# A pre-LN attention and SwiGLU block on one core: two-part opening, normalising tile by tile behind an estimated end, Newton steps in one piece, and which engine copies the last query block and the row sums

## The chip, the core and the metric

The program runs on one core of a Trainium2 chip. Its engines work in parallel, each through a queue of its own in program order: PE (TensorE, matrix products; PEld is its loading of stationary operands), DVE (VectorE), ACT (ScalarE), POOL (GpSimd) and SP (SyncE, which here only issues DMAs). They wait for each other through semaphores. The metric is device time in microseconds (us) of one execution; less is better. A row that begins with L99 tells of line 99 of the kernel.

## The reference

A transformer block on 2048 tokens of width 640, with 32 heads of 20 and a feed-forward width of 1728, all in fp32:

```
def _A_ref(x, wqkv, wo):
    qkv = (x @ wqkv).reshape(B, S, 3, H, Dh).transpose(2, 0, 3, 1, 4)
    q, k, v = qkv[0], qkv[1], qkv[2]
    p = softmax(einsum("bhqd,bhkd->bhqk", q, k) * Dh ** -0.5)
    o = einsum("bhqk,bhkd->bhqd", p, v)
    return o.transpose(0, 2, 1, 3).reshape(B, S, D) @ wo
def _B_ref(x, w_gate, w_up, w_down):
    return (silu(x @ w_gate) * (x @ w_up)) @ w_down
h  = x + _A_ref(layernorm(x), A_wqkv, A_wo)
h2 = h + _B_ref(layernorm(h), B_w_gate, B_w_up, B_w_down)
```

## The kernel before

Tokens are cut into four chunks of 512 (`c`, `NC = 4`), a chunk into four tiles of 128 (`TPC = 4`), the heads into eight groups of four (`g`, `NG = 8`). fp32 products are made of three products of rounded parts: each operand is split into `hi` (a rounded copy) and `lo` (the rest), and hi·hi, hi·lo and lo·hi are summed in PSUM. A `split` is therefore one copy (ACT) and one subtraction (DVE or POOL).

**Stage 1, projections** (to about 324 us). For each chunk: layer norm of four token tiles, turning them (`flip`) to put the features on the partitions, then ten query and key blocks and eight value blocks. A block is `rounds` (L594): 15 products of 64 rows each and, 20 products later, their 15 other halves. Between the rounds `visit` slips in other work by a model of the engines' clocks (`clock`, advanced by `takes` with estimated ns): chiefly the *early maxima* (`max_four`, L212, L224, L234), which compute row maxima of scores that the softmax needs and would else have to be made later; they read keys and queries back from DRAM into `raw` tiles. A maximum's reduction on DVE frees one of the five PSUM banks that its products use, and PE's queue is in order: a late reduction holds PE up.

The layer norm of chunk c+1 runs inside the blocks of chunk c as a list of steps `lns`, made by `norm`: four `stats` (two bn_stats and one bn_aggr on DVE), the reciprocal square root by three Newton steps (`rstd_steps`: two guess operations on DVE, twelve small ones, two to a list entry, on POOL), then four `apply` (L501, DVE), which normalise a tile in place. `norm_step` takes one entry from the list; it is called at most once per `visit` while `steps_due` lasts, and in a loop at the start of each block. When the last POOL entry has been issued, `x_there` is set to the estimated end of the chain plus `CHAIN` (3000 ns), and no entry is taken before that time of the model. POOL's queue also holds the splits of query and key blocks and the DMAs that store them (L566), from which SP's loads of `raw` (L152) follow.

For chunk 0 nothing can run ahead: the norm is written out in order (four stats, 14 Newton operations on DVE, four `apply`), then the turning (`flip_tokens`, L555), and the first two blocks (`first_blocks`, L647) in pieces of 256 columns. Before it PE does three products that nobody reads (L747), on the last x tile. `fill_ones` (L141) sets rows of the stacked keys to one on POOL. The last query block of chunk 3 is copied from PSUM by ACT (L679), split by ACT and POOL and stored through SP.

**Stage 2, attention** (to about 1460 us): 32 units `u` (group and chunk), each 16 key tiles `kt`. Per kt: four score products (`ps_one`, L1217, four banks in turn), four exponentials on ACT (L1223), eight products with the values into `acc` (L1227, called W here), and, while any are left, three late maxima (L245 on PE, L251 on DVE). W lags two kt behind the scores. After a unit's last W, `row_sums` copies `acc` to SBUF: 384 of 512 columns on ACT (L1238), then 128 on DVE (L1239). `acc` has one bank, so the next unit's first W waits for both.

**Stage 3**: output projection and the feed-forward part; its norms use the same `rstd_steps`, taken five (`moments`) or seven (`late_tokens`) operations at a time.

## Time and profile before

| what | us |
|---|---|
| runs: median (lowest to highest of 3) | 2030.67 (2030.37 to 2032.34) |
| the profiled execution | 2030.02 |
| its span, first to last instruction | 2028.2 |
| PE busy in the span | 2003.0 |
| mean granted PE clock | 0.999 |

The profile follows one execution. Busy times are unions of an engine's records. PE's matmuls are pipelined and their ends are modelled, so that PE can be told busy while it is held up for a few tenths of a us; starts of successive matmuls are the finer measure. The windows view gives, for each stretch of time, its length, each engine's busy time with the number of instructions, then the granted clock, the busy share of the DMA engines and GB/s. The waits view reads: who waited for whom, us in total, times, longest. The timeline reads: start, length, engine, line, operation, output and inputs, shapes, number merged, and in brackets the engine's idle time before it and what ended it.

### The profile page before, as it was taken

What the parts mean: (1) busy time and instruction counts of PE and PEld (TensorE: products, weight loads), DVE (VectorE), ACT (ScalarE), POOL (GpSimd) and SP (SyncE); (2) the same over time, 40 slices, a digit from 0 to 9 for tenths busy, and PEclk for the clock granted to TensorE, in tenths of its full rate; (3) what the DMA queues carried; (4) which work ended last, traced back from release to release, by engine and by line L of the source; (5) the groups of instructions that cost most, each with busy time, mean ns of one, the idle gap of its engine ahead of it and who ended that gap; (6) DMA issues with size and microseconds to landing.
All of it is one profiled execution on the core that took longest, in us unless ns stands there. A gap on an engine that the chain in (4) does not pass through costs nothing.

```text
span 2028.2 us, 40006 instructions
## 1 busy us (share of the span) xinstructions
PE 2003.0 (99%) x14300; PEld 1249.2 (62%) x14300; DVE 1610.5 (79%) x2858; ACT 1436.5 (71%) x2828; POOL 785.9 (39%) x1152
## 2 busy tenths in 40 slices
PE   8999999999999999999999999999999999999998
PEld 6989996333343433443333443345598888888888
DVE  5677778888999898989998989876388666676677
ACT  4677778999999999999999999987634222212221
POOL 6464423343352444343500011011146444844555
PEclk9999999999999999999999999999999999999999
DMA  7787563443534544535512132221158654974642
GB/s 243 245 254 260 175 209 83 127 138 105 184 109 126 164 128 131 160 122 175 158 49 78 28 83 61 87 62 55 51 194 296 216 185 158 354 266 155 205 149 93
DMA packets 199343, 310.38 MB, mean 153 GB/s; under 512 B 53744, under 2 KB 87856, under 8 KB 198120
## 3 DMA queue, kind: packets, MB, share of 16 engines
q1 hardware_dynamic: 192552, 284.21, 43.4%
q0 software_dynamic: 6496, 23.60, 4.0%
q8 instruction: 114, 1.87, 0.4%
q14 instruction: 85, 0.70, 0.1%
q10 hardware_dynamic: 96, 0.00, 0.0%
HBM read 208.11 MB, written 99.19 MB: 152 GB/s over the span
## 4 chain that ended last, share of the span: by engine, by line
PE 89%; DVE 1%; DMA 1%; issue 1%; ACT 1%; SPq 0%; POOL 0%; DVEq 0%; ACTq 0%; POOLq 0%
PE acc L1227 25%; PE ps_a L1397 15%; PE ps_one L1217 15%; PE ps_max L245 13%; PE ps_b L1491 8%; PE ps_one L594 6%; PE ps_max L212 2%; PE ps_max L948 2%; PE ps_b L948 2%; DMA halves<-j_d 1%; ACT probs L1223 0%; PE ps_max L983 0%; DVE tmp L1612 0%; SPq L1173 0%; SPq L297 0%
## 5 line engine op out<-in xcount | busy, mean ns | idle before, releaser
L1223 ACT ACTIVATE probs<-ps_one 128x512 f32<-128x512 f32 x2048 | 1058.0, 609 | 60.8 <-PE ps_one L1217 35.4
L251 DVE TENSOR_REDUCE mx<-ps_max 128x1 f32<-128x512 f32 x1472 | 924.9, 684 | 92.6 <-PE ps_one L1217 70.8
L1217 PE MATMUL ps_one<-q_stk,k_stk 62*128 62x512 f32 x2048 | 577.9, 447 | 1.0 <-ACT probs L1223 0.8
L1227 PE MATMUL acc<-probs,v_stk 128*32 128x512 f32 x4096 | 545.3, 605 | 1.0
L1217 PEld LDWEIGHTS ps_one<-q_stk,k_stk 62*128 62x128 f32 x2048 | 249.2, 184 | 436.9 <-ACT probs L1223 408.4
L245 PE MATMUL ps_max<-k_stk,q_stk 60*128 60x512 f32 x1472 | 371.6, 425 | 0.0
L245 PEld LDWEIGHTS ps_max<-k_stk,q_stk 60*128 60x128 f32 x1472 | 271.9, 186 | 22.4 <-DVE mx L251 0.9
L1612 DVE TENSOR_TENSOR tmp<-ps_a,tmp 128x512 f32<-128x512 f32 x208 | 141.2, 689 | 120.3 <-PE ps_a L1397 94.6
L234 DVE TENSOR_REDUCE mx<-ps_max 128x2 f32<-128x512 f32 x288 | 180.4, 685 | 66.9 <-PE ps_max L212 63.7
L1227 PEld LDWEIGHTS acc<-probs,v_stk 128*32 128x32 f32 x4096 | 80.7, 108 | 181.6 <-issue 167.1
L224 ACT ACTIVATE ps_max<-ps_max 128x512 f32<-128x512 f32 x288 | 151.7, 584 | 48.4 <-PE ps_max L212 45.6
L1491 PE MATMUL ps_b<-halves,yp 128*128 128x320 f32 x1032 | 179.3, 309 | 2.0 <-DMA halves<-j_d 1.3
L1491 PEld LDWEIGHTS ps_b<-halves,yp 128*128 128x128 f32 x1032 | 165.2, 188 | 18.6 <-POOL yp L90 1.5
L1397 PE MATMUL ps_a<-t,units 128*128 128x512 f32 x624 | 162.7, 396 | 0.2 <-ACT tmp L1625 0.2
L1397 PE MATMUL ps_a<-z,units 128*128 128x512 f32 x516 | 133.9, 394 | 0.0
L90 POOL TENSOR_TENSOR yp<-y,yp 128x256 fp32r<-128x256 f32 x96 | 60.2, 628 | 188.5 <-ACT yp L89 180.2
L1397 PEld LDWEIGHTS ps_a<-t,units 128*128 128x128 f32 x624 | 112.6, 188 | 19.0 <-ACT tmp L1625 0.5
L1264 POOL TENSOR_TENSOR o<-o,rb 128x512 f32<-128x512 f32 x31 | 39.9, 1286 | 199.2 <-DMA q_stk<-m_d 63.5
L1496 DVE TENSOR_TENSOR h<-ps_b,h 128x320 f32<-128x320 f32 x248 | 110.1, 481 | 7.1 <-PE ps_b L1491 5.4
L594 PE MATMUL ps_one<-z_hi,w_lo 64*128 64x512 f32 x380 | 112.6, 393 | 0.0
L594 PE MATMUL ps_one<-z_hi,w_hi 64*128 64x512 f32 x380 | 111.9, 393 | 0.0
L594 PE MATMUL ps_one<-z_lo,w_hi 64*128 64x512 f32 x380 | 111.4, 392 | 0.0
(215 smaller groups left out, 2644.8 us busy)
## 6 DMA issues: line engine op xcount, KB each, us to landing
units<-w_d SPq DMA_DIRECT2D x186, 256.0 KB
w_d<-stage SPq DMA_DIRECT2D x106, 256.0 KB
halves<-j_d SPq DMA_DIRECT2D x70, 320.0 KB
j_d<-stage SPq DMA_DIRECT2D x42, 320.0 KB
k_stk<-k_d SPq DMA_DIRECT2D x64, 160.0 KB
q_stk<-q_d SPq DMA_DIRECT2D x64, 160.0 KB
raw<-k_d SPq DMA_DIRECT2D x62, 160.0 KB
raw<-q_d SPq DMA_DIRECT2D x54, 160.0 KB
```

The costliest lines, as they stand in the source:

```text
L224: nc.scalar.activation(ps, ps, AF.Relu)
L234: nc.vector.tensor_reduce(mx[:, b, :, t, kc], ps.rearrange("p (j n) -> p j n", j=2), axis=AX.X, op=ALU.max,)
L245: nc.tensor.matmul(ps, queries[u][rows, pair, t * P : (t + 1) * P], keys[u // NC][rows, pair, kc * CH : (kc + 1) * CH], start=True, stop=True,
L251: nc.vector.tensor_reduce(mxs[u][:, b, pair, t, kc : kc + 1], ps, axis=AX.X, op=ALU.max)
L594: nc.tensor.matmul(ps, a[rows], b[rows], start=(i == n == 0), stop=(i == 1 and n == last), skip_group_check=True,)
L1217: nc.tensor.matmul(ps, keys[u // NC][rows, p, kt * P : (kt + 1) * P], queries[u][rows, p, :], start=True, stop=True,)
L1223: nc.scalar.activation(probs[p][:, b, :], ps, AF.Exp, scale=scale)
L1227: nc.tensor.matmul(acc[32 * j : 32 * j + 32, :], values[u // NC][:, kt, j * VW : j * VW + 32], probs[j // 2][:, j % 2, :], start=(kt == 0) ...
L1397: nc.tensor.matmul(ps.rearrange("p (t n) -> p t n", t=TPC), w[k][:, i], z[k][:, :, j], start=(first and m == 0), stop=(last and m == len(n ...
L1491: nc.tensor.matmul(ps, a, b, start=(n == 0), stop=(n == len(pairs) - 1))
L1496: nc.vector.tensor_tensor(out=h, in0=ps, in1=h, op=ALU.add)
L1612: add = lambda out, ps, x: nc.vector.tensor_tensor(out=out, in0=ps, in1=x, op=ALU.add)
```

## The change

1. **Opening.** The norm of chunk 0 is made for two halves of two tiles. On DVE: stats of tiles 0 and 1, their Newton steps threaded between the stats of tiles 2 and 3 (`between`); the Newton steps of tiles 2 and 3 go to POOL. Then PE turns tiles 0 and 1, computes columns 0 to 255 of the first two blocks for two of the three products, turns tiles 2 and 3, and does the rest. There are four products for nobody on x tile 0 where there were three on tile 3. One of the two halves of the ones is set by DVE and ACT where POOL did both.
2. **Newton steps.** On DVE one is three operations where it was four (a constant is folded into the guess); on POOL it is as before. `norm` uses POOL for all.
3. **One piece.** When `norm_step` meets a POOL entry it takes all POOL entries at once; `CHAIN` is 5000. The loop at a block's start becomes one step at most. `flip` of a chunk first takes what is left of the list.
4. **Normalising** (`norm_tokens`) for chunks 1 to 3 writes into another tile, whose five pieces of 128 columns lie 129 apart; there are five x tiles where there were four.
5. `LATE` is 4: weight blocks 4 and 5 have their `lo` made by POOL instead of DVE. `AFTER` (5, 6) puts one set of early maxima before group 7's.
6. The **last query block** is copied from PSUM by DVE and split by POOL alone.
7. **Row sums:** ACT copies all 512 columns.
8. Tiles for maxima of later units come from three buffers in turn.

```diff
+        if engine is nc.vector:
+            first = [
+                some(ts, v, var, EPS, -0.5, op0=ALU.add, op1=ALU.mult),
+                some(
+                    ts, r.bitcast(I32), v.bitcast(I32), -0.5, 519526879.0, op0=ALU.mult, op1=ALU.add
+                ),
+            ]
+            again = [
+                some(tt, out=t, in0=r, in1=r, op=ALU.mult),
+                some(tt, out=t, in0=t, in1=v, op=ALU.mult),
+                some(engine.scalar_tensor_tensor, r, t, 1.5, r, op0=ALU.add, op1=ALU.mult),
+            ]
+            return r, first + again * 3
...
-    def stats(pool, src, mv):
+    def stats(pool, src, mv, between=()):
         st = pool.tile([P, 2, 6], F32, name="st")
+        between = list(between)
         for i in range(2):
             nc.vector.bn_stats(st[:, i, :], src[:, i * HALF : (i + 1) * HALF])
+            if between:
+                between.pop(0)()
         nc.vector.bn_aggr(mv, st)
+        for f in between:
+            f()
...
+            if b and others:
+                others[0].memset(ones[:, 0], 1.0)
+                nc.scalar.activation(k[rows, 1], ones[:, 0], AF.Copy)
+            else:
+                nc.gpsimd.memset(ones, 1.0)
...
-        AFTER = 5, 7
+        AFTER = 5, 6
-        LATE, CHAIN = 6, 3000
+        LATE, CHAIN = 4, 5000
...
             takes(engine, ns, clock["PE"])
-            if engine == "POOL" and lns[0][0] == "DVE":
+            if lns and lns[0][0] == "POOL":
+                while lns[0][0] == "POOL":
+                    _, ns, f = lns.pop(0)
+                    f()
+                    takes("POOL", ns, clock["PE"])
                 x_there[0] = max(clock["PE"], clock["POOL"]) + CHAIN
...
+        def norm_tokens(tile, mv, r, t):
+            old = new = xs[tile]
+            if tile >= TPC:
+                old = old.rearrange("p (k n) -> p k n", k=ND)
+                new = xs[tile] = x_tile().rearrange("p (k n) -> p k n", k=ND)[:, :, :P]
+            nc.vector.tensor_scalar(
+                new, old, mv[:, t, 0:1], r[:, t : t + 1], op0=ALU.subtract, op1=ALU.mult
             )
...
             else:
-                nc.scalar.activation(copy[:, :CH], ps, AF.Copy)
+                if sync:
+                    nc.vector.tensor_copy(copy[:, :CH], ps)
+                else:
+                    nc.scalar.activation(copy[:, :CH], ps, AF.Copy)
...
+                    if sync:
+                        nc.gpsimd.tensor_copy(hi[:, :n], copy[:, :n])
+                        nc.gpsimd.tensor_tensor(
+                            out=lo[:, :n], in0=copy[:, :n], in1=hi[:, :n].bitcast(F32),
+                            op=ALU.subtract,
+                        )
+                        return
...
+        for _ in range(4):
+            nc.tensor.matmul(warm, ident, xs[0][:, :CH], start=True, stop=True)
+        r1, steps = rstd_steps(pa, mv[:, :2, 1], 2, "b")
+        r2, others = rstd_steps(pa, mv[:, 2:, 1], 2, "c", nc.gpsimd)
+        for t in range(2):
+            stats(pa, xs[t], mv[:, t, :])
+        for f in steps[:3]:
             f()
+        stats(pa, xs[2], mv[:, 2, :], steps[3:7])
+        stats(pa, xs[3], mv[:, 3, :], steps[7:])
+        for f in others:
+            f()
...
+        first_hi(0)
+        for t in range(2):
+            norm_tokens(t, mv, r1, t)
+            flip_tokens(t)
+            flipped_hi(t)
+        first_hi(1)
+        flipped_lo(0)
+        flipped_lo(1)
+        first_lo(0)
+        first_blocks((0, 0), (0, 1))
+        for t in range(2, TPC):
+            norm_tokens(t, mv[:, 2:], r2, t - 2)
+            flip_tokens(t)
+            flipped_hi(t)
...
                 if clock["PE"] >= x_there[0]:
-                    while steps_due[0] and lns:
-                        steps_due[0] -= 1
+                    if steps_due[0] and lns:
                         norm_step()
...
-        most = 3 * P
-        nc.scalar.activation(o[:, :most], acc[:, :most], AF.Copy)
-        nc.vector.tensor_copy(o[:, most:], acc[:, most:])
+        nc.scalar.activation(o, acc, AF.Copy)
```

What the planner makes of it stands in the engines' orders. First DVE, in the middle of chunk 0's blocks, from the sum over the last key block (`e`) to the early maxima (`mx`); L501 and, in the change, L551 are the normalising of chunk 1's tiles. Before:

```order
L684 TENSOR_TENSOR e_165<-e_165 128x256
L501 TENSOR_SCALAR xt<-xt,mv,r_a 128x640 x4
L234 TENSOR_REDUCE mx_131<-ps_max 128x2 x8
L234 TENSOR_REDUCE mx_135<-ps_max 128x2 x8
L234 TENSOR_REDUCE mx_139<-ps_max 128x2 x8
```

and in the change:

```order
L737 TENSOR_TENSOR e_150<-e_150 128x256
L551 TENSOR_SCALAR xt<-xt,mv,r_a 128x5x128 x3
L261 TENSOR_REDUCE mx_130<-ps_max 128x2 x4
L551 TENSOR_SCALAR xt<-xt,mv,r_a 128x5x128
L261 TENSOR_REDUCE mx_130<-ps_max 128x2 x4
```

Four normalisings ahead of the maxima became three, with the fourth behind two pairs of maxima. For chunks 2 and 3 every one of the four stands alone between maxima in the change.

Second POOL at the same time: the Newton operations of chunk 1 (`t_a`, `r_a`) and the splits and stores (DMA rows) of blocks. Before:

```order
L99 TENSOR_TENSOR r_a<-r_a,t_a 128x4
L90 TENSOR_TENSOR z_lo<-z_lo 128x256
L566 DMA k_d_63<-z_lo 16x2x768
L566 DMA k_d_63<-z_lo 80x2x768
L566 DMA k_d_63<-z_lo 32x2x768
L99 TENSOR_TENSOR t_a<-r_a 128x4
L99 TENSOR_TENSOR t_a<-t_a,v_a 128x4
L566 DMA q_d_59<-e_164 16x2x512
```

and in the change:

```order
L99 TENSOR_TENSOR r_a<-r_a,t_a 128x4
L99 TENSOR_TENSOR t_a<-r_a 128x4
L99 TENSOR_TENSOR t_a<-t_a,v_a 128x4
L99 TENSOR_SCALAR t_a<-t_a 128x4
L99 TENSOR_TENSOR r_a<-r_a,t_a 128x4
L90 TENSOR_TENSOR z_lo<-z_lo 128x256
L615 DMA k_d_63<-z_lo 16x2x768
```

The rows shown in the change are the end of twelve in a row; the split of `z_lo` and its stores stand behind all twelve, where they stood behind four.

Third DVE at the passage from stage 1 to stage 2: the last early maxima (`mx_129`), then the first late ones (`mx_128`). Before:

```order
L234 TENSOR_REDUCE mx_129<-ps_max 128x2 x12
L90 TENSOR_TENSOR m_5512<-ps_max,m_5512 16x128
L234 TENSOR_REDUCE mx_129<-ps_max 128x2 x4
L251 TENSOR_REDUCE mx_128<-ps_max 128x1 x31
```

and in the change:

```order
L90 TENSOR_TENSOR m_5191<-ps_max,m_5191 16x128
L261 TENSOR_REDUCE mx_143<-ps_max 128x2 x14
L261 TENSOR_REDUCE mx_129<-ps_max 128x2 x14
L730 COPY e_150<-ps_one 128x512
L261 TENSOR_REDUCE mx_129<-ps_max 128x2 x2
L280 TENSOR_REDUCE mx_128<-ps_max 128x1 x31
```

The finish of unit 0's maxima (`m`) moved up by a good twenty reductions, the copy of the last query block joined DVE's queue, and a pair of early maxima stands behind it.

More of the change, by code (lines that the diff above doesn't have):

```diff
@@ L171, in load_values, with mx_tile @@
         )
-    mxs = {u: stk.tile([P, 2, 2, TPC, NC], F32, name=f"mx{u}") for u in range(NU)}
+    def mx_tile(u, **tag):
+        return stk.tile([P, 2, 2, TPC, NC], F32, name=f"mx{u}", **tag)
+    mxs = {u: mx_tile(u) for u in range(NU) if u % NC < 2 or u == 2}
     clock = dict.fromkeys(("PE", "ACT", "DVE", "POOL"), 0)
@@ L496, in norm @@
             mv = pa.tile([P, TPC, 2], F32, name="mv")
[L497 to L504 removed]
+            r, steps = rstd_steps(pa, mv[:, :, 1], TPC, "a", nc.gpsimd)
             return (
@@ L520, in flip @@
             if n == 0:
+                while lns:
+                    norm_step()
                 zs[c] = z_tiles(c)
@@ L741, in tile_block @@
         load_x(0)
-        fill_ones(k_stk[0])
+        fill_ones(k_stk[0], nc.vector)
         for i in range(4):
```

67 lines of the change are left out of this document (35 added, 32 removed).

## The prediction

> **What bounds the kernel now.** The page first, then the windows view by stage (us and busy time of PE, PEld, DVE, ACT, POOL), then PE's waits in stage 1.
>
> ```profile
> PE 2003.0 (99%) x14300; PEld 1249.2 (62%) x14300; DVE 1610.5 (79%) x2858; ACT 1436.5 (71%) x2828; POOL 785.9 (39%) x1152
> ...
> 22.00:324.00 302.00, 296.28 (x3379) 279.83 (x3377) 214.69 (x365) 219.57 (x427) 152.20 (x210) 0.99 0.72 228
> 324.00:1460.00 1136.00, 1133.99 (x7884) 469.69 (x7883) 980.45 (x1686) 1074.87 (x2111) 328.37 (x524) 1.00 0.35 107
> ...
> PE ps_two L747 <- DMA xt<-in_A_x: 7.9, 1, 7.9
> PE ps_max L212 <- DVE mx L234: 4.6, 3, 2.4
> PE ps_max L212 <- ACT ps_max L224: 0.8, 2, 0.5
> ```
>
> PE is busy for 99% of the span, so an edit earns only where PE stands still, or where another engine holds up the start of its matmuls without the busy time showing it. In stage 1 PE stands still for 302.00 − 296.28 = 5.7 us, most of it in three waits for reductions of the early maxima. The opening, the passage to stage 2 and the 31 changes of unit are the other places. All sums below are made against the profiled execution, 2030.02 us; the median of the runs shown is 0.65 us above it.
>
> **The norms of chunks 1 to 3.** DVE and PE at chunk 1, a window at the slow clock behind it, and all sixteen normalisings (shortest, median, longest ns):
>
> ```profile
> 58.75 5.01 DVE L501 TENSOR_SCALAR xt<-xt,mv,r_a 128x640 f32<-128x640 f32 x4 [1.68 <-POOL r_a L99]
> 64.41 0.39 PE L212 MATMUL ps_max<-raw 60*128 60x256 f32 x2 [2.40 <-DVE mx L234]
> 66.00:70.00 4.00, 4.00 (x45) 4.00 (x43) 1.44 (x3) 2.01 (x4) 2.63 (x4) 0.60 0.90 323
> ...
> L501 DVE TENSOR_SCALAR xt<-xt,mv,r_a x16: 602/606/2101, 11.7 to 213.6; 128x640 f32<-128x640 f32 x16
> ...
> 50.48 0.20 POOL L99 TENSOR_TENSOR t_a<-r_a 128x4 f32<-128x4 f32 x1
> 51.32 0.20 POOL L99 TENSOR_TENSOR r_a<-r_a,t_a 128x4 f32<-128x4 f32 x1
> 19.54 3.02 DVE L90 TENSOR_TENSOR w_lo<-raw,w_hi 128x640 fp32r<-128x640 f32 x4
> ```
>
> DVE waits 1.68 us for the last Newton operation, then four normalisings take 5.01 us (twice the 4 × 0.606 that they need at the median), and the maxima behind them come late: PE stands still for 2.40 us. Then the granted clock falls to a mean of 0.60 over 4 us with PE busy throughout, which is 4 × 0.40 = 1.6 us of lost work. In the change the twelve Newton operations run in one piece. The first four start from 50.48 to 51.32, 0.28 us apart, so twelve take 3.4 us and end near 53.9; DVE asks at 58.75 − 1.68 = 57.07. The normalisings write five pieces. The trace has none of that form: the lower bound is 0.606, the upper the longest seen, 2.101; I take 0.76, from the four subtractions of 128x640 in 3.02 us, the nearest DVE row of that size. Three in a row are then 2.3 us, ahead of maxima that were held up for 1.68 + 5.01 = 6.7. The 4.4 us gained exceed the 2.40 that PE waited, so the wait goes and the slow clock with it: **−2.4 and −1.6**. What is late next would be the banks behind the three normalisings: 2.3 us of DVE against 1.9 in the planner's estimate, hidden by the reductions that PE has already queued.
>
> On the form: the Trainium skill (VectorE: DVE Perf Modes, Mode 2×_2P) says that this mode needs outermost sizes that are even or equal in source and destination, which five pieces out of a plain row of 640 would not be; and (SBUF — State Buffer, two separate sides) that an operation in that mode and a GpSimd one exclude each other for their whole length. The spread from 602 to 2101 ns agrees with such exclusion; by these pages the new form costs about 0.76 and never waits.
>
> Chunks 2 and 3, by the same views:
>
> ```profile
> 126.56 1.53 DVE L501 TENSOR_SCALAR xt<-xt,mv,r_a 128x640 f32<-128x640 f32 x1 [2.63 <-POOL r_a L99]
> 124.00:130.00 6.00, 4.10 (x42) 3.45 (x38) 3.44 (x5) 3.03 (x7) 5.04 (x9) 1.00 0.89 306
> 203.00:206.00 3.00, 2.70 (x30) 2.35 (x28) 2.01 (x5) 2.27 (x5) 0.46 (x3) 1.00 0.80 264
> 103.00:112.00 9.00, 8.34 (x77) 7.24 (x75) 8.86 (x20) 6.67 (x12) 5.53 (x6) 1.00 0.78 221
> ```
>
> At 126 DVE waits 2.63 us for a Newton chain that POOL had been given in pieces between stores; the first normalising now stands eight reductions later on DVE, some 5 us, and the chain is whole: PE's 6.00 − 4.10 = 1.9 us go, **−1.9**. At 203 the same in small, **−0.3**. At 103 to 112 three stats in a row hold reductions up and PE loses 9.00 − 8.34 = 0.66; the change takes one stat at a time, but that stretch has ACT waits too: between 0 and −0.66, I take **−0.3**. `LATE` gives POOL two subtractions near 20 us, while it waits for the first blocks; at nothing, since DVE's next work there waits for PE. The AFTER order and the later tiles for maxima move no work into a wait that I can find: nothing, with ±1 for what a planner does elsewhere.
>
> **The opening.**
>
> ```profile
> 1.38 7.05 POOL L141 MEMSET k_stk<- 32x4096 f32 x2
> 3.83 0.89 DVE L125 BATCH_NORM_STATS2 st<-xt 128x6 f32<-128x320 f32 x2 [2.95 <-DMA xt<-in_A_x]
> 6.78 0.89 DVE L125 BATCH_NORM_STATS2 st<-xt 128x6 f32<-128x320 f32 x2 [0.83 <-DMA xt<-in_A_x]
> 8.94 0.17 DVE L99 TENSOR_SCALAR v_a<-mv 128x4 f32<-128x4 f32 x1
> 11.74 2.18 DVE L501 TENSOR_SCALAR xt<-xt,mv,r_a 128x640 f32<-128x640 f32 x4
> 12.40 1.86 PE L555 MATMUL ps_wide<-ident,xt 128*128 128x128 f32 x15
> 7.89 4.45 PE L747 MATMUL ps_two<-xt,ident 128*128 128x512 f32 x6 [7.89 <-DMA xt<-in_A_x]
> 22.41 1.43 PE L594 MATMUL ps_one<-z_hi,w_hi 64*128 64x512 f32 x5
> ```
>
> Tile 0 lands at 3.83, tile 2 at 6.78. The ones on DVE (half of what POOL does in 3.5 us, so below 1.8 at its rate) lie before 3.83, their copy on ACT before its first turned tile is there: no cost. From 6.78 DVE now does four bn_stats (0.89 a pair), two aggregates (0.1) and ten small operations (0.2 each, as 14 fill 8.94 to 11.74): 1.8 + 0.2 + 2.0 = 4.0, so the first normalising starts near 10.7, not 11.74, and PE turns from 11.4, not 12.40. But PE's 10.0 us from there to 22.41 grow: its first product needs the turned tile 1 and the second weight block, both through ACT, at about 13.4, so some 0.6 of the 1.0 is given back: **−0.4**, bounds 0 and −1.0. A caution: the four idle products, at 4.45 / 3 each from 3.83, end by 9.8, sooner if the clock rises, and PE then stands still for 1.6 us or more; at chunk 1 a stop of 2.40 brought the slow clock. If it falls here, 1.6 are lost again.
>
> The Trainium skill (TensorE: Matmul & The Clock Gate, Why this matters for your kernels) has the clock fall only for gaps beyond about 3 us. The fall behind 2.40 us differs from it, and the measurement decides; by the page this loss has no chance, and −0.4 stands.
>
> **The changes of unit.** One boundary on PE (W rows), ACT and DVE, and the waits of W for the copy:
>
> ```profile
> 838.03 1.06 PE L1227 MATMUL acc<-probs,v_stk 128*32 128x512 f32 x8
> 840.15 1.07 PE L1227 MATMUL acc<-probs,v_stk 128*32 128x512 f32 x8
> 842.38 1.07 PE L1227 MATMUL acc<-probs,v_stk 128*32 128x512 f32 x8
> 844.60 1.06 PE L1227 MATMUL acc<-probs,v_stk 128*32 128x512 f32 x8
> ...
> 839.56 2.07 ACT L1223 ACTIVATE probs<-ps_one 128x512 f32<-128x512 f32 x4
> 841.48 0.53 ACT L1238 ACTIVATE o<-acc 128x384 f32<-128x384 f32 x1
> 841.85 2.66 ACT L1223 ACTIVATE probs<-ps_one 128x512 f32<-128x512 f32 x5
> 842.04 0.29 DVE L1239 COPY o<-acc 128x128 f32<-128x128 f32 x1 [0.35 <-ACT o L1238]
> ...
> PEld acc L1227 <- DVE o L1239: 13.5, 29, 0.5
> ```
>
> A kt takes 840.15 − 838.03 = 2.12 us; the two around a boundary take 2.23 and 2.22, so each of 29 boundaries costs 0.21. Two things meet there. W waits for the DVE part, which ends at 842.33. And ACT is full: four exponentials fill 839.56 to 841.48, 0.48 each, leaving 2.12 − 1.92 = 0.20 per kt for a copy that takes 841.85 − 841.48 = 0.37. ACT falls 0.17 behind, the fourth score finds its bank still in use, and the next W is late. The change ends the first wait: 512 columns are done by about 842.1, before W's turn at 842.27. It deepens the second: the copy takes 0.48, ACT falls 0.28 behind. If ACT decides, 0.21 becomes 0.31, 29 × 0.1 = +2.9; if W's wait decided, 842.38 − 842.27 = 0.11 goes, −3.2; if all goes, −6.1. Since the second late kt is explained by ACT alone, I take **+2.9**. This edit is the one that speaks against the change.
>
> **The passage to stage 2, and the end of attention.**
>
> ```profile
> 324.19 0.60 ACT L679 ACTIVATE e<-ps_one 128x512 f32<-128x512 f32 x1 [2.08 <-POOL e L90]
> 325.36 2.04 ACT L1223 ACTIVATE probs<-ps_one 128x512 f32<-128x512 f32 x4
> 325.99 0.98 PE L1217 MATMUL ps_one<-q_stk,k_stk 62*128 62x512 f32 x2 [0.83 <-ACT probs L1223]
> 1464.04 1.00 PE L948 MATMUL ps_b<-wo_hi,o_hi 128*128 128x320 f32 x5 [1.07 <-DVE o L1239]
> ```
>
> Without the copy and split of the last query block (324.19 to 325.36) ACT could begin its exponentials up to 1.2 us earlier. But DVE now has that copy (about 0.7) and a pair of early maxima (1.3) behind it, and PE's first late maxima need their banks: from −1.2 to +0.5, I take **−0.2**. At 1464 PE waits 1.07 for ACT's and then DVE's share of the last sums; without the second, **−0.3**. The feed-forward part has three norm operations fewer in each chain and begins its late tokens one step earlier: nothing.
>
> Sum: −2.4 − 1.6 − 1.9 − 0.3 − 0.3 − 0.4 + 2.9 − 0.2 − 0.3 = −4.5, so 2030.02 − 4.5 = **2025.5 us**; bounds of the terms carry it from about 2022 to 2028.5.
>
> **Rivals.** *The unit change gains.* W's wait goes and ACT's lag is absorbed by the four banks: −3.2 in place of +2.9, 2025.5 − 6.1 = 2019.4. For it: DVE's 0.29 lies in series on W's wait, 29 times. Against: the row at 841.85 shows ACT without a pause. *The stalls move.* The planner's clocks err elsewhere, PE finds new waits of 2 us twice, half of the 6.5 of the norms' gain comes back and the idle opening drops the clock (1.6): 2025.5 + 3.2 + 1.6 = 2030.3. For it: the planner was 4 us wrong at chunk 1. *The one piece stops POOL (slower).* Twelve operations, 3.4 us, stand ahead of the splits and stores of two blocks, and SP's loads of `raw` follow those stores:
>
> ```profile
> SPq L152 <- POOL t_a L99: 3.6, 1, 3.6
> ```
>
> SP has waited 3.6 us for such operations once already. If a load lands later than the planner's due time, PE stands for up to 3.4 and the clock falls for 1.6 more, 5.0 a chunk; two chunks would give 2035.5, three 2040.5. It decides once the delay exceeds the slack in the landing times; against it, PE's waits now name no `raw` transfer at all.
>
> **Chances.** Forecast 0.44 (its own range 2022 to 2028.5); the unit change gains 0.18; the stalls move 0.26; POOL stopped 0.12. No more than 0.2% (4.06 us, what a measurement of this kernel can hardly tell from nothing) off 2030.67 is 2026.6 to 2034.7. Of the forecast some three quarters lie below 2026.6 (0.33), all of the second (0.18) and a little of the third (0.03): faster 0.54, same 0.34, slower 0.12. For the range I reach down into the second case and up over the third: 2018.5 to 2031.5.
>
> **What would show it.** Right: no PE wait on L261 above 1 us near 60 and 126; clock 1.00 there; normalisings of 128x5x128 near 0.76 us with no long ones; PE's turning from 11.4; first W of units 2.12 after the one before, but the second W about 2.43 after it. Wrong: W intervals at boundaries of 2.12 twice (second case); PE waits for `raw` (fourth); a granted clock of one half near 11 to 15.

## The result and the profile after

The changed kernel takes 2025.84 us (median of 5 runs, 2022.30 to 2026.28), the kernel before 2032.19 on the same chip (5 runs, 2030.37 to 2033.13): a ratio of 0.9966, 95% interval 0.9955 to 0.9977. It is faster by 0.34%, and the interval lies beyond the 0.2% that the prediction asked for. Predicted were 2025.5 us. The prediction stood against earlier runs of the kernel before (2030.67); beside the changed kernel that kernel was 1.5 us slower, so the medians differ by 6.35 us. In the two profiled executions the span goes from 2028.2 to 2024.0.

The page's busy times and the windows of the two large stages after the change (columns as before):

```profile
PE 2003.7 (99%) x14302; PEld 1242.0 (61%) x14302; DVE 1602.4 (79%) x2816; ACT 1439.9 (71%) x2827; POOL 788.5 (39%) x1166
...
22.00:324.00 302.00, 297.38 (x3393) 279.09 (x3395) 219.69 (x370) 223.49 (x435) 158.23 (x217) 1.00 0.72 228
324.00:1460.00 1136.00, 1134.55 (x7892) 463.13 (x7884) 971.43 (x1647) 1074.83 (x2107) 324.15 (x520) 1.00 0.35 106
```

PE's busy total hides the gain, as it hid the loss: it does the same products, and stands still for less. PE's waits after the change (total, times, longest):

```profile
PE ps_two L805 <- DMA xt<-in_A_x: 4.3, 1, 4.3
...
PE ps_max L569 <- DVE xt L551: 1.8, 2, 1.0
...
PE ps_max L274 <- DVE mx L261: 0.9, 1, 0.9
PE ps_max L239 <- ACT ps_max L251: 0.9, 2, 0.6
...
PE ps_one L1300 <- DMA q_stk<-m_d: 0.6, 1, 0.6
PE ps_max L239 <- DVE mx L261: 0.4, 1, 0.4
```

The last row was the largest of stage 1 before (4.6 us, L212 <- L234). In its place stands a smaller new one: the flips (L569, turning of the next chunk) wait 1.8 us for normalised tiles. DVE and PE around the first of them:

```profile
57.55 0.93 DVE L551 TENSOR_SCALAR xt<-xt,mv,r_a 128x640 f32<-128x640 f32 x1
60.08 1.92 DVE L551 TENSOR_SCALAR xt<-xt,mv,r_a 128x640 f32<-128x640 f32 x2 [1.60 <-issue]
61.91 2.47 DVE L261 TENSOR_REDUCE mx<-ps_max 128x2 f32<-128x512 f32 x4
64.30 0.93 DVE L551 TENSOR_SCALAR xt<-xt,mv,r_a 128x640 f32<-128x640 f32 x1
...
65.29 0.53 PE L569 MATMUL ps_max<-ident,xt 64*128 64x64 f32 x10 [1.05 <-DVE xt L551]
```

The reductions no longer wait behind four normalisings; the fourth normalising now waits behind four reductions, and the flip with it. DVE waits no more for POOL's Newton operations. One boundary of units, with ACT's whole copy:

```profile
835.04 1.06 PE L1310 MATMUL acc<-probs,v_stk 128*32 128x512 f32 x8
836.38 0.63 ACT L1320 ACTIVATE o<-acc 128x512 f32<-128x512 f32 x1
837.16 1.06 PE L1310 MATMUL acc<-probs,v_stk 128*32 128x512 f32 x8
839.02 0.18 PEld L1300 LDWEIGHTS ps_one<-q_stk,k_stk 62*128 62x128 f32 x1 [0.31 <-ACT probs L1306]
839.45 1.07 PE L1310 MATMUL acc<-probs,v_stk 128*32 128x512 f32 x8
841.56 0.64 PE L1310 MATMUL acc<-probs,v_stk 128*32 128x512 f32 x4
```

W follows after 2.12, 2.29 and 2.11 us, where it took 2.12, 2.23 and 2.22: the first late step is gone, the second is longer. What holds it is a score's bank that ACT still reads (839.02).

Where the 4.24 us between the two spans went, from the starts of the same instructions in both traces:

| stretch | before, us | after, us | difference |
|---|---|---|---|
| start to the first 64-row product | 22.41 | 22.14 | −0.27 |
| from there to the first score | 300.90 | 297.10 | −3.80 |
| first score to first W | 4.67 | 4.47 | −0.20 |
| first W to that of unit 30 | 1032.97 | 1032.21 | −0.76 |
| unit 30 | 57.30 | 58.56 | +1.26 |
| the rest | 609.99 | 609.52 | −0.47 |

Two of these are not of any edit that can be pointed at: a query load (L1300 <- DMA above) makes one step at unit 17 0.85 us longer, inside the −0.76, and in unit 30 PE's clock drops:

```profile
1392.00:1394.00 2.00, 2.00 (x9) 0.21 (x9) 0.53 (x2) 1.78 (x4) 0.00 (x0) 0.61 0.00 0
1394.00:1396.00 2.00, 2.00 (x16) 0.70 (x12) 0.00 (x0) 1.09 (x3) 0.00 (x0) 0.53 0.00 0
```

The third column from the right is the granted clock. This half clock lasts some 3.4 us, as the one at 66 did in the kernel before; here it costs the 1.26 of unit 30.

### The profile page after: what moved, and what is told of

Same layout as the page of the kernel before. It is cut to its first block, busy times and chain, and to the rows that moved or that the text cites. A ratio compares the mean times of both kernels' runs of the same rounds, so it can differ in the third digit from the quotient of the medians.

```text
span 2024.0 us, 39916 instructions
## 1 busy us (share of the span) xinstructions
PE 2003.7 (99%) x14302; PEld 1242.0 (61%) x14302; DVE 1602.4 (79%) x2816; ACT 1439.9 (71%) x2827; POOL 788.5 (39%) x1166
## 3 DMA queue, kind: packets, MB, share of 16 engines
q8 instruction: 114, 1.87, 0.4%
## 5 line engine op out<-in xcount | busy, mean ns | idle before, releaser
L1300 PE MATMUL ps_one<-q_stk,k_stk 62*128 62x512 f32 x2048 | 583.3, 450 | 0.7 <-DMA q_stk<-m_d 0.6
L1300 PEld LDWEIGHTS ps_one<-q_stk,k_stk 62*128 62x128 f32 x2048 | 248.7, 184 | 441.2 <-ACT probs L1306 416.7
```

The lines of the kernel that those rows point to most:

```text
L1300: nc.tensor.matmul(ps, keys[u // NC][rows, p, kt * P : (kt + 1) * P], queries[u][rows, p, :], start=True, stop=True,)
```

## Experiments

Twelve kernels. All ratios are to the kernel before, timed beside them on the same chip (2031.44, 2031.70 and 2032.50 us beside the first, second and last four rows); the changed kernel's is 0.9966. Stages and waits are read from one profiled execution of each kernel, and single executions of one kernel differ: the five of the changed kernel lie between 2022.30 and 2026.28.

| kernel | median, us | ratio, 95% |
|---|---|---|
| before, ACT copies the sums | 2031.33 | 0.9999 (0.9990 to 1.0007) |
| changed, DVE copies the sums | 2024.51 | 0.9963 (0.9951 to 0.9975) |
| changed, norms undone | 2027.19 | 0.9974 (0.9965 to 0.9982) |
| changed, rows of 640 | 2022.90 | 0.9957 (0.9945 to 0.9969) |
| changed, opening undone | 2028.84 | 0.9981 (0.9972 to 0.9990) |
| changed, three idle products | 2025.18 | 0.9964 (0.9952 to 0.9977) |
| changed, last block by ACT | 2023.92 | 0.9959 (0.9947 to 0.9972) |
| changed, rows, short gap | 2023.01 | 0.9957 (0.9944 to 0.9969) |
| changed, Newton in pairs | 2040.11 | 1.0036 (1.0022 to 1.0049) |
| changed, all steps that are due | 2035.42 | 1.0010 (1.0001 to 1.0020) |
| changed, four edits together | 2025.65 | 0.9960 (0.9948 to 0.9973) |
| changed, again | 2025.17 | 0.9963 (0.9950 to 0.9975) |

### The copy of the sums by ACT alone, in the kernel before

```
-        nc.scalar.activation(o[:, :most], acc[:, :most], AF.Copy)
-        nc.vector.tensor_copy(o[:, most:], acc[:, most:])
+        nc.scalar.activation(o, acc, AF.Copy)
```

> The kernel before, with ACT copying all 512 columns of the last sums and DVE none; nothing else is changed. Theory A (the forecast: ACT alone decides a unit's late start, all of the 0.21 grows with its lag): first W of a unit 2.12 after the one before, second W 2.43; each of 29 boundaries 0.10 dearer, the span 2.9 us longer than before's 2028.2. Theory B (two separate waits: the first late step, 0.11, was W's wait for DVE's part and goes; the second, 0.10, is ACT's lag and grows as the lag does, 0.28/0.17 = 1.65 times): 2.12 and then 2.28 to 2.29, each boundary 0.05 cheaper, the attention part 1.4 us shorter, stage 1 unchanged with its stalls of 2.57 and 2.08 near 62 and 127.

PE's W rows and the copy at the same boundary of this kernel:

```profile
840.75 1.06 PE L1227 MATMUL acc<-probs,v_stk 128*32 128x512 f32 x8
842.09 0.63 ACT L1237 ACTIVATE o<-acc 128x512 f32<-128x512 f32 x1
842.87 1.06 PE L1227 MATMUL acc<-probs,v_stk 128*32 128x512 f32 x8
845.17 1.07 PE L1227 MATMUL acc<-probs,v_stk 128*32 128x512 f32 x8
```

2.12 and 2.30 here; over 29 boundaries the medians are 2.125 and 2.273, against 2.230 and 2.217 before. This is theory B, met to 0.02 us. The pair of steps is 0.05 shorter, and from the first W to unit 30 it takes 1031.99 in place of 1032.97, 0.98 of the 1.4 expected. A gain of 1 us in 2031 does not show in the times.

### The copy by DVE alone

```
-        nc.scalar.activation(o, acc, AF.Copy)
+        nc.vector.tensor_copy(o, acc)
```

> The changed kernel, with DVE copying all 512 columns of the last sums and ACT none. It takes 0.48 us of copy off ACT and puts about 0.7 on DVE at each change of unit. Theory B (the second late step is ACT's lag alone): that step falls back from 2.28 to 2.12 in every unit; the first W then waits for DVE, whose copy stands behind the reduction already begun and takes about 0.7: 2.12 plus 0 to 0.7. If on average 0.3, attention is 29 x (0.3 - 0.16) = 4 us longer than in the changed kernel. Theory C (the second late step is not ACT's lag but comes from the change of keys and queries, or from the maxima): it stays near 2.28 whoever copies, and attention is longer by 29 x 0.3 = 9 us. In both DVE's own late maxima can hold PE up further, DVE being busy 95% of that stage.

The steps are 2.173 and 2.217 (medians), neither theory's figure. The first W waits only 0.05, since DVE begins the copy (0.68 us) soon after the last W. And the second step is late without any copy on ACT, by 0.09 against a step of 2.127 inside a unit, where it is 0.15 in the changed kernel. At 838.42 the load of a late maximum's weights is released by DVE's reduction, which fits a DVE that has fallen behind by the copy; that this alone makes the step late is not shown. So theory C's claim (late whoever copies) holds in part, and how much of the lateness elsewhere is ACT's lag stays open. The 95% in the expectation is ACT's share of the stage (1074.83 of 1136.00 us in the changed kernel); DVE's is 971.43, or 86%. The pair takes 4.39 against 4.40 in the changed kernel: it matters little who copies, as long as it is one.

### The norms of chunks 1 to 3 undone

```
-            if lns and lns[0][0] == "POOL":
-                while lns[0][0] == "POOL":
...
+            if engine == "POOL" and lns[0][0] == "DVE":
                 x_there[0] = max(clock["PE"], clock["POOL"]) + CHAIN
...
-                    if steps_due[0] and lns:
+                    while steps_due[0] and lns:
+                        steps_due[0] -= 1
                         norm_step()
...
-        LATE, CHAIN = 4, 5000
+        LATE, CHAIN = 4, 3000
...
-            if tile >= TPC:
-                old = old.rearrange("p (k n) -> p k n", k=ND)
-                new = xs[tile] = x_tile().rearrange("p (k n) -> p k n", k=ND)[:, :, :P]
```

> The changed kernel with the norms of chunks 1 to 3 as before: Newton operations given to POOL in pairs, normalisings in place in one go, the gap of 3000 ns; the opening, the sums and the last query block stay as changed. Theory A (the norms' edits are what shortened stage 1 by 3.8 us after the opening): PE waits of 2 us or more for reductions come back once or twice, with a slow clock behind at least one of them; from the first 64-row product to the first score some 301 us in place of 297.1; the span 3 to 5 us longer than the changed kernel's 2024.0. Theory B (the stalls were chance of one order, and any other order would have removed them): no wait above 1 us for a reduction, stage 1 within 1 us of the changed kernel's.

From DVE's rows and PE's waits of this kernel:

```profile
57.33 5.54 DVE L544 TENSOR_SCALAR xt<-xt,mv,r_a 128x640 f32<-128x640 f32 x4 [1.48 <-POOL r_a L99]
62.78 2.47 DVE L261 TENSOR_REDUCE mx<-ps_max 128x2 f32<-128x512 f32 x4
...
PE ps_max L239 <- DVE mx L261: 4.9, 3, 2.7
```

All that the prediction read in the trace of before is back: the wait for POOL, four normalisings in a row, the waits of PE (it stands for 2.87 at 60.65 and 2.06 at 126.44), and half clock from 62 to 69. Stage 1 after the opening takes 301.76 us against 297.10: theory A, 4.7 us for these edits, of which the half clock, 6.83 us long, is about 3. The whole shows less: the span is 2026.4, 2.4 above the changed kernel's, since in this execution the opening is 1.07 shorter and unit 30 has no half clock, and the median, 2027.19, is 1.4 to 2.0 above, with overlapping intervals.

### Only the Newton operations in pairs, and only all steps that are due

Two kernels, each with one half of the norms' edits taken back: the first has the first hunk above alone, the second the second alone. Both keep the gap of 5000 and the five pieces.

> The changed kernel, but the Newton operations of chunks 1 to 3 go to POOL in pairs as the planner's clock allows, as before; normalising stays one tile at a time, with five-piece rows and the gap of 5000 ns. The last pair is later, so the gap ends after the flips are due, and all four normalisings are flushed in a row just ahead of them. Theory A (the one piece is what removed the stalls): the flips wait for four in a row, 4 x 0.93 = 3.7 us of DVE, so PE stands for 2 to 4 us at each of chunks 1 and 2 with the clock at half behind it, and stage 1 after the opening takes 301 to 304 us in place of 297.1. Theory B (taking one tile at a time is what removed them): waits no longer than now (1.24 and 0.94 us), 297 to 298 us.

> The changed kernel, but at each slot the planner gives all norm steps that are due, as before, not one; the Newton operations stay in one piece. Chunk 1 keeps its order; in chunk 2 the first normalising follows the Newton steps at once and the others stand 4 to 5 rows earlier on DVE. Theory A (the one piece suffices): no wait for reductions above 1 us, stage 1 after the opening 296.5 to 297.5 us. Theory B (the spacing counts): DVE stands still for POOL's Newton operations at chunk 2 (about 3.4 us for twelve, against the first normalising right behind them), reductions behind it come late, PE waits 1.5 us or more near 125, and stage 1 takes 298.5 to 301.

PE's waits in the first, then in the second, and DVE in the second:

```profile
PE ps_max L565 <- DVE xt L547: 8.2, 10, 1.2
```

```profile
PE ps_max L239 <- DVE mx L261: 8.7, 2, 5.5
```

```profile
108.43 0.17 DVE L99 TENSOR_SCALAR r_a<-v_a 128x4 int32<-128x4 int32 x1
113.25 0.94 DVE L551 TENSOR_SCALAR xt<-xt,mv,r_a 128x640 f32<-128x640 f32 x1 [4.65 <-POOL r_a L99]
114.10 0.41 DVE L737 TENSOR_TENSOR z_hi<-z_hi 128x256 f32<-128x256 f32 x1
114.44 2.48 DVE L261 TENSOR_REDUCE mx<-ps_max 128x2 f32<-128x512 f32 x4
```

With pairs the last Newton step is so late that the normalisings are still undone when the flips are due, at all three chunks: stage 1 after the opening takes 312.58 us, far above the 301 to 304 expected, with 6.8 and 3.4 us of half clock behind the first two. With all due steps at once, DVE is given the first normalising right behind twelve Newton operations that POOL has not begun; it stops 4.65 us, the reductions with it, and PE 5.5: stage 1 takes 309.64 us, with nearly 7 us of half clock behind each of two such stops. In stage 1 each half alone is 15.5 and 12.5 us worse than both together, and worse than neither (301.76); the medians, 2040.11 and 2035.42, say the same. The one piece is only good with the wait behind it, and the wait only with the one piece. The rival in which one piece makes the kernel slower is right about the piece by itself, though the queue that suffers is DVE's, not SP's.

### Rows of 640 in place of five pieces

```
-            if tile >= TPC:
-                old = old.rearrange("p (k n) -> p k n", k=ND)
-                new = xs[tile] = x_tile().rearrange("p (k n) -> p k n", k=ND)[:, :, :P]
...
-                            xs[c * TPC + t][rows, k], ident[rows, rows],
+                            xs[c * TPC + t][rows, k * P : (k + 1) * P], ident[rows, rows],
```

> The changed kernel, but the normalisings of chunks 1 to 3 write in place, rows of 640, as before, at the new place in the order. Theory A (the form sets the price): the twelve fall from 0.93 to 0.606 us at the median, and some of them take up to 2.1 us again, where GpSimd works at the same time; the flips' waits for them (1.24 and 0.94 us) shrink by about 0.3 each unless a long one falls there, so the span is 0 to 1 us shorter, or up to 2 us longer. Theory B (the price is of the place in the program and not of the form): the twelve stay near 0.93, with none above 1 us, and the time does not move.

The twelve normalisings of the changed kernel and of this one (shortest, median, longest ns), and in this one the row that has the longest with the POOL row beside it:

```profile
L551 DVE TENSOR_SCALAR xt<-xt,mv,r_a x12: 929/930/940, 57.5 to 212.3; 128x640 f32<-128x640 f32 x12
```

```profile
L548 DVE TENSOR_SCALAR xt<-xt,mv,r_a x12: 602/604/1390, 56.5 to 210.5; 128x640 f32<-128x640 f32 x12
...
129.22 1.29 POOL L90 TENSOR_TENSOR v_stk<-v_stk 128x512 fp32r<-128x512 f32 x1 [0.66 <-ACT v_stk L89]
129.46 1.39 DVE L548 TENSOR_SCALAR xt<-xt,mv,r_a 128x640 f32<-128x640 f32 x1
```

Theory A: the form sets the price. In the changed kernel the same normalising, at 130.91, runs in 0.93 in the middle of the same POOL subtraction (130.66 to 131.96). The Trainium skill (SBUF — State Buffer, two separate sides) has such a DVE operation and a GpSimd one exclude each other; the row of 1.39 agrees. It ends 0.35 us after POOL's, as the three long rows of the kernel before do (0.35 or 0.36), so part of the 0.60 is done by then. The five-piece form escapes it, as the Trainium skill (VectorE: DVE Perf Modes, Mode 2×_2P) lets one expect of five pieces out of a row of 640. But the escape costs 0.33 us twelve times, more than the exclusion does (11.2 us for the twelve against 8.2). Why the form takes 0.93 and not a subtraction's 0.755 stays open: the five pieces and the 129 columns between them were never changed apart. The waits of the flips shrink to 1.1, and stage 1 takes 296.27: in these traces the padding, for itself, is a loss of 0.8 us.

### Rows and the short gap

In addition to the last edit:

```
-        LATE, CHAIN = 4, 5000
+        LATE, CHAIN = 4, 3000
```

> The changed kernel with two edits: normalisings in place by rows of 640 (0.604 us at the median against 0.93), and the gap ahead of the normalisings 3000 ns in place of 5000, so that the four of chunk 1 follow each other and the last of chunk 2 stands one pair of reductions earlier. Theory A (the flips wait only because the last normalising stands behind reductions): the two waits left in the kernel with rows alone (0.7 and 0.4 us of PE, gaps of 0.87 and 0.65) go, no wait for a reduction above 0.5 us comes, stage 1 after the opening takes 296.3 - 1.5 = 294.8, the span 1 to 1.5 us below that kernel's. Theory B (any earlier normalising holds up reductions as in the kernel before): a wait for reductions of 1 us or more comes near 60 or 125, with a slow clock behind it when it is long, and stage 1 takes 297 or more.

No flip waits any more, and no reduction holds PE for over 0.5 us, as theory A has it. But in this execution a load for the early maxima came late:

```profile
PE ps_max L239 <- DMA raw<-q_d: 2.1, 1, 2.1
PE ps_max L239 <- ACT ps_max L251: 1.2, 3, 0.6
PE ps_max L239 <- ACT e L572: 0.9, 1, 0.9
```

with half clock around 186: stage 1 took 300.33. The median is that of the rows alone (2022.90 and 2023.01), so the gap is worth nothing that can be measured.

### The opening undone, and three idle products

The first puts the opening of before into the changed kernel; of its edit

```
-        for _ in range(4):
-            nc.tensor.matmul(warm, ident, xs[0][:, :CH], start=True, stop=True)
+        for _ in range(3):
+            nc.tensor.matmul(warm, ident, xs[TPC - 1][:, :CH], start=True, stop=True)
...
+        for t in range(TPC):
+            stats(pa, xs[t], mv[:, t, :])
+        for f in steps:
+            f()
+        for t in range(TPC):
+            norm_tokens(t, mv, r, t)
```

The second is

```
-        for _ in range(4):
+        for _ in range(3):
             nc.tensor.matmul(warm, ident, xs[0][:, :CH], start=True, stop=True)
```

> The changed kernel with the opening of before (ones by GpSimd, three idle products on tile 3, one Newton run of 14 small operations, four normalisings in a row, blocks in the old order); all else as changed. Read from the landing of x's first tile to the first 64-row product: before 18.58, the kernel before with ACT's copy 19.5, the changed kernel 17.9, three kernels with its opening 16.8 to 17.1. Theory A (the forecast: 0.4 gained, since most of the earlier normalising is given back): 17.5 to 18.4 here, the span within 0.5 us of the changed kernel's usual. Theory B (the opening is worth more: the forecast let the first products wait, but they start with two tiles turned): 18.5 to 19.5 here, the span 1.5 to 2 us longer. The moment at which the clock opens moves either by about 1 us from run to run.

> The changed kernel with three idle products in place of four. In the changed kernel's profile the first normalising waited 1.01 us for the last of them, and 0 to 0.2 in three kernels where the clock opened earlier. Theory A (the fourth product is only in the way): the first normalising starts 0 to 1.0 us earlier against the landing of tile 0, and the clock stays open in the longer stop of PE; the time is 0 to 1 us shorter. Theory B (the prediction's caution: PE's idle stop drops the clock or lets it open later): turning and the first products run at half clock for up to 3.4 us, and the first 64-row product is 1 to 2 us later.

DVE and PE in the opening of the changed kernel, then of the kernel with rows of 640, whose opening is the same:

```profile
4.29 6.53 PE L805 MATMUL ps_two<-xt,ident 128*128 128x512 f32 x8 [4.29 <-DMA xt<-in_A_x]
10.87 1.14 DVE L551 TENSOR_SCALAR xt<-xt,mv,r_b 128x640 f32<-128x640 f32 x2 [1.01 <-PE ps_two L805]
11.53 1.31 PE L596 MATMUL ps_wide<-ident,xt 128*128 128x128 f32 x10 [0.71 <-DVE xt L551]
22.14 1.43 PE L643 MATMUL ps_one<-z_hi,w_hi 64*128 64x512 f32 x5
```

```profile
4.18 5.67 PE L802 MATMUL ps_two<-xt,ident 128*128 128x512 f32 x8 [4.18 <-DMA xt<-in_A_x]
9.90 1.13 DVE L548 TENSOR_SCALAR xt<-xt,mv,r_b 128x640 f32<-128x640 f32 x2 [0.17 <-PE ps_two L802]
10.56 1.32 PE L593 MATMUL ps_wide<-ident,xt 128*128 128x128 f32 x10 [0.71 <-DVE xt L548]
21.15 1.43 PE L640 MATMUL ps_one<-z_hi,w_hi 64*128 64x512 f32 x5
```

The four idle products take 6.53 us in the one and 5.67 in the other, because the clock opens later in the first (the traces record it as full from 10.05 and from 8.22); DVE is ready at 9.86 there and waits for them, since the normalising overwrites the tile that they read. From the landing of tile 0 to the first 64-row product it takes 18.59, 19.53 and 18.02 us with the old opening (the last is the undone one), and with the new one 17.95 and 17.77 in the two profiles of the changed kernel and 16.80 to 17.08 in seven other kernels. The 18.02 lies in theory A's range, but the changed kernel's usual figure is below what A took it for: the means, 18.71 of three and 17.16 of nine, are 1.5 us apart, nearer to B. Single executions differ by 1 us, so the worth of the opening stays between 0.1 (18.02 against 17.95) and 1.6. Part of it may be the clock's: it is full 2.9 to 5.9 us after tile 0 has landed in the new opening and 6.5 to 9.4 in the old, whose idle products wait for tile 3; no run changes that alone. The median with the opening undone is 3 us higher, not all of which is the opening's: that kernel's profile also has a late load (1.1 us of PE at 68) and two half clocks. With three idle products it took 16.80, and the clock did not fall in the stop: theory A, with a gain of 0 to 1.1 against the kernels with four that the times don't show (2025.18).

### The last query block by ACT

```
-                if sync:
-                    nc.vector.tensor_copy(copy[:, :CH], ps)
-                else:
-                    nc.scalar.activation(copy[:, :CH], ps, AF.Copy)
+                nc.scalar.activation(copy[:, :CH], ps, AF.Copy)
```

and its split by ACT and POOL, as before.

> The changed kernel with the last query block copied and split by ACT, as before. From the first score to the first W the kernels without this edit took 4.67 and 4.64 us, those with it 4.47, 4.49, 4.46 and 4.28. Theory A (the forecast's -0.2 is of this edit): 4.65 here, the span 0.2 us longer, and 0.9 us of PE's wait for the last early maxima (behind DVE's copy) goes, while ACT's first exponentials start up to 1.2 later. Theory B (the passage is set by the early maxima alone): 4.2 or less here, the span 0.3 to 0.5 us shorter than the changed kernel's usual. A difference of this size is read from the trace, not from the times.

4.01 us from the first score to the first W, against 4.47: theory B. Ten kernels with the copy on DVE took 4.26 to 4.51, so in this one profile giving it to DVE costs 0.25 to 0.5, since it stands ahead of the last reductions there; PE's wait for these falls from 0.9 to 0.5. The first step of unit 0 then took 3.70 in this execution, at half clock; that came in other kernels too (next section), so it is not put to this edit.

### Four edits together, and the changed kernel once more

Rows of 640, `CHAIN` 3000, three idle products, and DVE's copy of the sums; beside it the changed kernel unchanged.

> The changed kernel with four edits that single runs spoke for: normalisings in place by rows of 640, a gap of 3000 ns, three idle products, and DVE copying the last sums whole. Expected from those runs against the changed kernel: stage 1 after the opening 295.5 in place of 297.1, the opening 16.8 from the landing of the first tile in place of 17.0, a pair of late steps at each unit 4.39 in place of 4.40 and steps between them 0.02 shorter, 0.7 in all: 2.5 us less, a median near 2022 and a ratio of 0.9950 to the kernel before. Rival: loads of the early maxima come late in some executions whenever the order is moved (2.1 us of PE in the profile of the kernel with rows and the short gap), and the median is no better than 2024.

> The changed kernel unchanged, profiled once more, to tell what of its first profile was of that execution alone: the clock that opened at 10.05, the wait of 0.85 us for a query load at unit 17, and the half clock of 3.41 us at 1392. Theory A (they are chance): opening 16.8 to 17.1 from the landing of the first tile to the first 64-row product in place of 17.95, no half clock at 1392, a span of 2021 to 2023. Theory B (they are of the change): the same three again, a span of 2024.

The four edits do not add up in the times: 2025.65, ratio 0.9960, the same as the changed kernel. Opening (16.80) and unit steps (4.40) are as expected, but a load is late again (1.4 us at 66), with half clock at 322 to 326. That is the rival. The smallest median of all is that of rows alone, 2022.90; the intervals overlap, so no version is shown to beat the changed kernel.

The second profile of the changed kernel shows what was of the first alone. It has full clock at 1392, and instead, behind the passage to stage 2:

```profile
322.00:324.00 2.00, 1.94 (x12) 0.66 (x12) 2.00 (x4) 1.84 (x4) 2.00 (x1) 0.82 0.60 125
324.00:326.00 2.00, 2.00 (x14) 0.85 (x7) 0.36 (x1) 0.21 (x1) 1.95 (x2) 0.50 0.88 277
326.00:328.00 2.00, 2.00 (x15) 0.61 (x13) 1.78 (x3) 1.85 (x4) 2.00 (x1) 0.83 0.33 111
```

Stage 1 is the same to 0.04 us (297.14), so its waits belong to the order; the half clock moves. The opening is late here too (17.77), and so is the step at unit 17 (3.08 us, 2.98 in the first profile); the theory of chance expected neither. Over the twelve profiles of changed kernels that step takes 2.12 to 3.49, and 2.13 and 2.59 in the two others: the query load behind it has little slack.

## Why the prediction was right, and where it was not

The time was met (2025.5 against 2025.84), its direction and the place of the gain too. That it was met within 0.4 us is luck: several terms were off by more and made up for each other.

- **Stalls of chunks 1 to 3** (−2.4, −1.6, −1.9, −0.3 and −0.3, together −6.5): the reading is right. The waits for reductions at 60 and 126 and the half clock behind the first are gone, they come back when the edits are undone, and neither edit does it alone. The size was wrong by 2.7 us: −3.80. The step that failed is the one on what is late next: it looked only at the banks behind the three normalisings. The flips wait for the last normalising, which was moved behind reductions, 1.24 at 64 and 0.94 at 142 (from the end of the last product's columns to the next start). The stats at 103 to 112, taken at −0.3, gave nothing that can be seen: two successive starts on PE lie 0.67 and 0.99 us apart there (102.06 and 111.58), both waiting for ACT, where the longest distance before was 0.85 (104.47).
- **The new form**: 0.93 us, not 0.76, inside the bounds of 0.606 and 2.101. The row of a subtraction was the wrong neighbour. That it never takes a long time was right (929 to 940 ns).
- **Changes of unit** (+2.9): the sign was wrong; 29 × (4.399 − 4.445) = −1.3 by the mean steps of the two traces. The prediction had named both waits rightly and then let ACT's lag scale the whole 0.21, though 0.11 of it was W's wait for DVE, which goes. Scaled alone, 0.10 × 0.28 / 0.17 = 0.165, where 0.155 is measured, and the second W comes after 2.29 us, not 2.43. The run with this edit alone shows the sign and, to 0.02, the steps; that the second step is ACT's lag alone is not shown, since it is late by 0.09 with no copy on ACT.
- **Opening** (−0.4): −0.27 in that profile, where tile 0 landed 0.35 us later than before; against the landing −0.64, and about −1.5 between the means of all profiles. The 0.6 given back between turning and the 64-row product is right (10.0 before, 10.61 after). What was mis-sized is the start: DVE is ready at 9.86, not 10.7: from 6.83 its work takes 3.03 us, not 4.0, as the ten small operations, set among the bn_stats and aggregates, add 0.10 each and not 0.2. PE still turns from 11.53 (11.4 forecast), because the idle products end at 10.82, not by 9.8, and DVE waits 1.01 for them. The caution of a falling clock did not come true.
- **Passage** (−0.2): −0.20. But it was not the copy on DVE that gave it; with that taken back alone, the first W comes 0.46 sooner. Which of the other edits did is not shown.
- **End of attention and the rest** (−0.3): −0.47.
- **Not foreseen**: +1.26 for a half clock at unit 30, +0.85 for a late query load. The slow clock was counted as gone with its stall; it came elsewhere.

The rival "the unit change gains" had the sign: W's wait goes, but ACT's lag is not absorbed, so −1.3 stands where it had −3.2. The rival "the stalls move" was right in kind and too large in size: the waits moved to the flips, with about a third of the gain, and the slow clock to other places. The rival on POOL's queue did not happen in the changed kernel: PE waits for no `raw` there. But the loads of the early maxima have little slack: in three kernels with moved orders they cost PE 1.1, 2.1 and 1.4 us.

## What to carry to other kernels

When two waits follow each other at one place, price the removed and the deepened one apart: the sum of both is not a number that either edit scales. When work is moved ahead of or behind a queue, follow both ends of it: what it held up, and who needs its result next, for that is where the stall goes. And two edits of a schedule may only work as a pair, so an undo of one half tells of the coupling and not of that half's worth.

## What the runs showed of the hardware

A half clock of PE (0.50 for 3.4 or 6.8 us) came ahead of the end in twelve of the fourteen profiled executions, one to three times in each: near 63 to 66, 112, 129, 151, 185, 194, 322 to 335 or 1391 to 1396. It also came behind much shorter stops than the one at chunk 1: at the passage it came behind stops of 1.10 and 0.38 us in the second execution of the changed kernel, and not in the first, whose stops there were the same. Only the kernels with DVE's copy and with three idle products had none before the end, in spans of 2020.3 and 2020.8. So a saved stall brings the half clock's 1.3 to 1.7 us for certain only if no other stop draws it. The Trainium skill (TensorE: Matmul & The Clock Gate, Why this matters for your kernels) ties the fall to gaps beyond about 3 us; these rows show it behind less, and not each time.

Part of the chance lies in a grid. In every trace the half clocks begin a whole number of steps of 3.413 us after the moment at which the clock became full (54.61 us or 16 steps in the kernel before, 1382.40 or 405 in the changed kernel, 314.03 or 92 in its second execution), and that moment moves between 6.64 and 13.12. In stage 1 of these fourteen traces it goes with how much of a stop falls into one step: every step in which PE's records leave 1.83 us or more idle is followed by a half clock, and no step at full clock with 1.70 or less is. Two steps each of the kernel before and of the kernel before with ACT's copy:

```profile
62.39:65.80 3.41, 1.39 (x22) 1.32 (x24) 3.41 (x5) 0.96 (x2) 2.19 (x3) 1.00 0.97 320
65.80:69.21 3.41, 3.41 (x38) 3.41 (x38) 1.64 (x3) 1.64 (x4) 1.92 (x3) 0.50 0.86 300
```

```profile
125.77:129.18 3.41, 1.54 (x17) 1.20 (x15) 2.78 (x4) 0.49 (x2) 3.00 (x7) 1.00 0.93 303
129.18:132.59 3.41, 3.41 (x24) 3.31 (x22) 1.94 (x4) 1.98 (x4) 0.41 (x1) 0.50 0.92 310
```

Both kernels stop at chunk 1 and at chunk 2 in the same order of work. In the first the stop at chunk 1 leaves one step 2.03 us idle, and the clock falls there; in the second the longer stop at chunk 1 (2.94) is split over two steps, 1.51 and 1.43, and the clock falls at chunk 2 instead, behind a step with 1.87. The half clocks at the passage and near 1392 stand behind steps with 1.05 us idle and less, so what draws those stays open.
